# Cross-attention feeding a snake feed-forward layer: state times w_in formed per batch, blocks cut by batch, second layer and attention interleaved by hand

## The chip, the cores and the metric

The kernel runs on one core of one Trainium2 chip. The metric is the device time in microseconds of one execution. Matmuls run on PE (TensorE), whose weight loads are shown apart as PEld; elementwise work runs on DVE (VectorE), ACT (ScalarE) and POOL (GpSimd); transfers are started from the queues of POOL and SP. Each engine works through its own list of instructions in order and waits on semaphores of the others.

## What is computed

There are 8 batches b of 8 heads h; x[b, h] has 512 tokens of 64 numbers, state[b, h] has 32 rows of 64. Per head, attention runs both ways with the same scores, and the 512 + 32 results of all 8 heads are laid side by side as rows of 512 numbers. These 4352 rows go through a two-layer network.

```python
scores = scale * np.matmul(x, state.transpose(0, 1, 3, 2))
a = softmax(scores)                 # over the 32 state rows
xread = np.matmul(a, state)         # 512 x 64 per head
a2 = softmax(scores^T)              # over the 512 tokens
sread = np.matmul(a2, x)            # 32 x 64 per head
X = concat([xread, sread], axis=2)  # to 4352 rows of 512
h = X @ w_in                        # 512 -> 2048
g = h + sin(alpha * h)**2 / (alpha + 1e-09)
out = g @ w_out                     # 2048 -> 512, f32
```

## The kernel before

Everything inside is bf16 with f32 accumulation. Heads are worked on in pairs (q = 0 to 3; 2 x 64 = 128 partitions). Tokens of a batch lie four to a partition, so a batch is C = 4 chunks of 128 tokens. The intermediate X is kept transposed for all batches in `xT_all` [128, 4, 4352].

Loads: `load_batch` casts x to bf16 in flight (one transfer per batch on POOL's queue) and lays the state of a head pair out as a block diagonal `stbd` (a memset and two transfers per batch). w_in and w_out come as one transfer each. Transfers on POOL's queue use eight semaphores in turn, so from the ninth on each waits for the one eight before it.

Attention of a pair: `a1_transposes` copies x into pair order (`xp`, L116), transposes it and the state on PE; `a1_scores` copies the transpose out of PSUM (`xbT`, L130), makes the scores (L133) and their Exp on ACT (`E`, L140). `a2_rows` sums rows of E and divides on DVE (`R` L148, `rR` L150, `A` L153) and transposes A; `a2_readout` multiplies the state with it (`U_ps`, L170) and ACT casts the result into `xT_all` (L171). `a2_sread` makes x times E and, with a matrix of ones, the column sums (L181, L187), and DVE reduces, inverts and multiplies (L195 to L205).

The network: `moe_block` takes 512 columns of `xT_all`, whatever batch they are from: 8 blocks of 512 and one of 256. For each of 16 column tiles ft of w_in it runs four matmuls over the 512 rows (`hT_ps`, L259), Sin on ACT (L266), the square on POOL for even ft and on DVE for odd (L271), and one DVE instruction that scales the square and adds h from PSUM (`gT`, L274). Then each 128 rows of the block take 16 matmuls with w_out (`o_ps`, L283), a copy on ACT (L290) and stores from SP's queue.

`attn_a1(b + 1)`, `attn_a2(b)` and a block are written one after the other; the order in each engine's list is set by a scheduler with a cost model, which fills some instructions of neighbouring stages into each other. The pools set what may run ahead: four PSUM buffers `psumM` for `hT_ps`, scores, `U_ps` and `WTC_ps` together, two for transposes, two for `o_ps`.

Of the kernel before, what the change touches and what calls it, by code (L numbers as in the profile page):

```python
# [9 lines left out]
ACT = mybir.ActivationFunctionType  # L10
ALU = mybir.AluOpType
AX = mybir.AxisListType
BF16 = mybir.dt.bfloat16
FP32 = mybir.dt.float32


@with_exitstack
def kernel(
# [27 lines left out]
    bload = ctx.enter_context(tc.tile_pool(name="bload", bufs=B))
    epool = ctx.enter_context(tc.tile_pool(name="epool", bufs=2 * Q))
    pairp = ctx.enter_context(tc.tile_pool(name="pairp", bufs=3))
    smallp = ctx.enter_context(tc.tile_pool(name="smallp", bufs=4))
    moep = ctx.enter_context(tc.tile_pool(name="moep", bufs=2))  # L50
    outp = ctx.enter_context(tc.tile_pool(name="outp", bufs=2))
    psumT = ctx.enter_context(tc.tile_pool(name="psumT", bufs=2, space=bass.MemoryType.PSUM))
    psumM = ctx.enter_context(tc.tile_pool(name="psumM", bufs=4, space=bass.MemoryType.PSUM))
    psumO = ctx.enter_context(tc.tile_pool(name="psumO", bufs=2, space=bass.MemoryType.PSUM))

    ident = const.tile([P, P], BF16, name="ident")
    make_identity(nc, ident[:])
# [11 lines left out]
    xT_all = xt_pool.tile([P, Q, T_TOTAL], BF16, name="xT_all")

    xnat_l = [None] * B
    stbd_l = [None] * B

    def load_batch(b):
        xnat = bload.tile([P, H, C * D], BF16, name="xnat")
        nc.gpsimd.dma_start(
            xnat[:], x[b].rearrange("h (p i) d -> p h (i d)", i=C)
        )
        stbd = bload.tile([Ns * 2, Q, 2 * D], BF16, name="stbd")
        nc.gpsimd.memset(stbd[:], 0.0)  # L80
        stv = state[b].rearrange("(q r) j d -> r j q d", r=2)
        for r in range(2):
            nc.gpsimd.dma_start(
                stbd[r * Ns:(r + 1) * Ns, :, r * D:(r + 1) * D],
                stv[r],
            )
        xnat_l[b] = xnat
        stbd_l[b] = stbd

    load_batch(0)  # L90
    load_batch(1)
    w_in_sb = wpool.tile([P, Q, DFF], BF16, name="w_in_sb")
    nc.gpsimd.dma_start(w_in_sb[:], moe_w_in.rearrange("(q p) f -> p q f", p=P))
    for b in range(2, B):
        load_batch(b)
    w_out_sb = wpool.tile([P, FT, DOUT], BF16, name="w_out_sb")
    nc.gpsimd.dma_start(w_out_sb[:], moe_w_out.rearrange("(ft p) c -> p ft c", p=P))

    BLK = 512
    nblocks = (T_TOTAL + BLK - 1) // BLK  # L100

    ps = {}

    def a1_transposes(b, q):
        d = {}
        ps[(b, q)] = d
        xnat = xnat_l[b]
        stbd = stbd_l[b]
        stbdT_ps = psumT.tile([P, 2 * Ns], BF16, name="stbdT_ps", tag="tp")
        nc.tensor.transpose(stbdT_ps[:], stbd[:, q, :], ident[:Ns * 2, :Ns * 2])  # L110
        stbdT = pairp.tile([P, 2 * Ns], BF16, name="stbdT")
        nc.vector.tensor_copy(stbdT[:], stbdT_ps[:])  # L112
        d["stbdT"] = stbdT
        xp = pairp.tile([P, C, 2 * D], BF16, name="xp")
        for r in range(2):
            nc.vector.tensor_copy(  # L116
                xp[:, :, r * D:(r + 1) * D],
                xnat[:, 2 * q + r, :].rearrange("p (i d) -> p i d", i=C),
            )
        xbT_ps = psumT.tile([P, S], BF16, name="xbT_ps", tag="tp")  # L120
        for i in range(C):
            nc.tensor.transpose(  # L122
                xbT_ps[:, i * P:(i + 1) * P], xp[:, i, :], ident[:]
            )
        d["xbT_ps"] = xbT_ps

    def a1_scores(b, q):
        d = ps[(b, q)]
        xbT = pairp.tile([P, S], BF16, name="xbT")
        nc.vector.tensor_copy(xbT[:], d["xbT_ps"][:])  # L130
        S_ps = psumM.tile([P, C, 2 * Ns], FP32, name="S_ps", tag="hT")
        for i in range(C):
            nc.tensor.matmul(  # L133
                S_ps[:, i, :],
                xbT[:, i * P:(i + 1) * P],
                d["stbdT"][:],
                start=True, stop=True,
            )
# [156 lines left out]
    for b in range(B):  # L295
        if b + 1 < B:
            attn_a1(b + 1)
# [38 lines left out]
```

## Time and profile before

| | us |
|---|---|
| median of 3 runs | 372.04 |
| lowest and highest | 369.31, 373.11 |
| span of the profiled execution | 371.1 |

The profiled execution is one by itself, recorded apart from the three timed runs; of its time only the span, from the first instruction to the last, is on record, and it lies within the range of the runs.

How to read the page: the first part gives each engine's busy time and share of the span. In the part of 40 slices, each 9.28 us long, a digit is the busy share in tenths; the GB/s row is what the transfers moved. The chain that ended last is followed back from the last instruction through whatever released each step. A row of the groups gives line, engine, operation, out<-in by name, shape and count, then busy time, mean ns of one, idle time just before and what ended it. A row of the timeline gives start, duration, engine, line, operation and count, and in brackets the idle time before it and its releaser. A row by line gives the smallest, median and largest duration in ns. A row of the windows gives the stretch, its length, the busy time of PE, PEld, DVE, ACT and POOL with counts, then the granted TensorE clock (1.00 is full), the share of the DMA engines and GB/s.

### The profile page before, as it was taken

The numbers are of one execution on the slowest core, as the hardware profiler recorded it, in microseconds if no ns is written. First come the engines' busy times: TensorE is split into PE (matmuls) and PEld (weight loads), VectorE is DVE, ScalarE is ACT, GpSimd is POOL, SyncE is SP. The second block draws the span as 40 slices with busy tenths as digits, with TensorE's granted clock in tenths as the row PEclk, the third lists the DMA queues.
The fourth block names the chain that finished last, engine by engine and source line by source line (L and its number), as shares of the span: only waits on it lengthen the run. The fifth ranks groups of instructions, "written<-read, shape, count | busy, mean of one in ns | idle before, by whom it ended". The sixth has DMA issues, their size and how long they took to land.

```text
span 371.1 us, 5139 instructions
## 1 busy us (share of the span) xinstructions
PE 314.4 (85%) x1830; PEld 150.6 (41%) x1856; DVE 232.9 (63%) x602; ACT 160.5 (43%) x256; POOL 96.8 (26%) x113
## 2 busy tenths in 40 slices
PE   0458799989997989789997989789997999799994
PEld 0343334544343434443354434443453434334561
DVE  2657675289818991679627990789437970695081
ACT  1113362366334651556334641556254642363271
POOL 9238242015200440024200530025100430152040
PEclk9999989999998999989998999989998999899999
DMA  9999930200030002200120002000120003101201
GB/s 93 211 194 188 196 54 31 83 4 0 8 91 17 2 0 57 59 0 3 28 85 2 0 0 87 28 2 0 41 75 0 3 2 83 30 0 25 71 20 57
DMA packets 20681, 17.90 MB, mean 48 GB/s; under 512 B 5552, under 2 KB 15792, under 8 KB 20656
## 3 DMA queue, kind: packets, MB, share of 16 engines
q0 software_dynamic: 13216, 8.65, 16.1%
q1 hardware_dynamic: 7440, 8.93, 8.7%
q8 instruction: 14, 0.23, 0.2%
q14 instruction: 11, 0.09, 0.1%
HBM read 17.31 MB, written 8.91 MB: 71 GB/s over the span
## 4 chain that ended last, share of the span: by engine, by line
PE 47%; DVE 26%; POOL 12%; issue 6%; DMA 4%; ACT 3%; POOLq 0%; ACTq 0%
PE o_ps L283 25%; PE hT_ps L259 11%; POOL s_sb L271 10%; DVE gT L274 10%; DMA stbd<-in_state_dram 4%; DVE xbT L130 3%; PE U_ps L170 2%; DVE recipC L197 2%; DVE A L153 2%; PE WTC_ps L181 2%; DVE s_sb L271 2%; PE xbT_ps L122 2%; PE WTC_ps L187 2%; ACT s_sb L266 2%; DVE xp L116 2%
## 5 line engine op out<-in xcount | busy, mean ns | idle before, releaser
L259 PE MATMUL hT_ps<-xT_all,w_in_sb 128*128 128x512 bf16 (+1 forms) x560 | 138.7, 385 | 14.8 <-DVE gT L274 11.6
L271 POOL TENSOR_TENSOR s_sb<-s_sb 128x512 bf16<-128x512 bf16 (+1 forms) x72 | 74.2, 1031 | 250.5 <-ACT s_sb L266 175.2
L283 PE MATMUL o_ps<-w_out_sb,gT 128*128 128x512 bf16 x534 | 126.6, 379 | 2.7 <-DVE gT L274 2.0
L266 ACT ACTIVATE s_sb<-hT_ps,alpha_sb 128x512 bf16<-128x512 f32 (+1 forms) x144 | 94.7, 663 | 57.8 <-PE hT_ps L259 27.3
L274 DVE SCALAR_TENSOR_TENSOR gT<-s_sb,inva_sb,hT_ps 128x512 bf16<-128x512 bf16 (+1 forms) x144 | 101.5, 714 | 25.8 <-POOL s_sb L271 20.8
L259 PEld LDWEIGHTS <-w_in_sb 128*128 128x128 bf16 x576 | 58.0, 102 | 82.8 <-issue 34.8
L283 PEld LDWEIGHTS <-gT 128*128 128x128 bf16 x544 | 52.1, 98 | 68.8 <-DVE gT L274 9.6
L290 ACT COPY o_sb<-o_ps 128x512 f32<-128x512 f32 x34 | 19.9, 586 | 90.0 <-PE o_ps L283 86.4
L112 DVE COPY stbdT<-stbdT_ps 128x64 bf16<-128x64 bf16 x32 | 5.8, 182 | 57.6 <-PE stbdT_ps L110 46.6
L271 DVE TENSOR_TENSOR s_sb<-s_sb 128x512 bf16<-128x512 bf16 (+1 forms) x72 | 29.0, 402 | 0.0
L171 ACT CAST xT_all<-U_ps 128x512 bf16<-128x512 f32 x32 | 18.4, 592 | 21.4 <-PE U_ps L170 15.2
L130 DVE COPY xbT<-xbT_ps 128x512 bf16<-128x512 bf16 x32 | 13.5, 423 | 18.8 <-PE xbT_ps L122 17.5
L170 PE MATMUL U_ps<-AT,stbd 64*128 64x512 bf16 x32 | 13.3, 427 | 12.5 <-DVE AT L168 12.4
L195 DVE TENSOR_REDUCE Csum<-WTC_ps 128x64 f32<-128x256 f32 x32 | 13.3, 422 | 16.2 <-PE WTC_ps L187 15.6
L110 PE MATMUL stbdT_ps<-ident,stbd 64*128 64x64 bf16 x32 | 6.5, 204 | 16.9 <-DMA stbd<-in_state_dram 16.9
L140 ACT ACTIVATE E<-S_ps 128x256 bf16<-128x256 f32 x32 | 10.3, 388 | 22.8 <-PE S_ps L133 22.7
L116 DVE COPY xp<-xnat 128x256 bf16<-128x256 bf16 x64 | 17.5, 327 | 3.8 <-DMA xnat<-in_x_dram 3.4
L153 DVE TENSOR_TENSOR A<-E,rR 128x256 bf16<-128x256 bf16 x32 | 18.8, 591 | 0.0
L122 PE MATMUL xbT_ps<-ident,xp 128*128 128x128 bf16 x128 | 14.6, 242 | 4.0 <-DVE xbT L130 3.7
L197 DVE RECIPROCAL recipC<-Csum 128x64 f32<-128x64 f32 x32 | 15.3, 519 | 0.1
L266 ACT ACT_TABLE_LOAD x7 | 9.0, 1283 | 13.9 <-PE hT_ps L259 13.8
L168 DVE COPY AT<-AT_ps 64x512 bf16<-64x512 bf16 x32 | 13.1, 414 | 2.7 <-PE AT_ps L158 2.2
(30 smaller groups left out, 150.3 us busy)
## 6 DMA issues: line engine op xcount, KB each, us to landing
xnat<-in_x_dram POOLq DMA_DIRECT2D x8, 512.0 KB, 9.1
out_dram<-o_sb SPq DMA_DIRECT2D x16, 192.0 KB, 2.2
w_in_sb<-in_moe_w_in_dram POOLq DMA_DIRECT2D x1, 2048.0 KB, 16.1
w_out_sb<-in_moe_w_out_dram POOLq DMA_DIRECT2D x1, 2048.0 KB, 14.7
out_dram<-o_sb SPq DMA_DIRECT2D x8, 256.0 KB, 2.4
out_dram<-o_sb SPq DMA_DIRECT2D x16, 128.0 KB, 2.3
out_dram<-o_sb SPq DMA_DIRECT2D x24, 64.0 KB, 1.9
stbd<-in_state_dram POOLq DMA_DIRECT2D x16, 16.0 KB, 8.6
```

The lines of the kernel that those rows point to most:

```text
L116: nc.vector.tensor_copy(xp[:, :, r * D:(r + 1) * D], xnat[:, 2 * q + r, :].rearrange("p (i d) -> p i d", i=C),)
L122: nc.tensor.transpose(xbT_ps[:, i * P:(i + 1) * P], xp[:, i, :], ident[:])
L130: nc.vector.tensor_copy(xbT[:], d["xbT_ps"][:])
L153: nc.vector.tensor_tensor(A8, E8, rR[:].unsqueeze(2).to_broadcast([P, C * 2, Ns]), ALU.mult)
L170: nc.tensor.matmul(U_ps[:], stbd[:, q, :], AT[:], start=True, stop=True)
L197: nc.vector.reciprocal(recipC[:], Csum[:])
L259: nc.tensor.matmul(hT_ps[:, :Nt], w_in_sb[:, q, ft * P:(ft + 1) * P], xT_all[:, q, t0:t0 + Nt], start=(q == 0), stop=(q == Q - 1),)
L266: nc.scalar.activation(s_sb[:, :Nt], hT_ps[:, :Nt], ACT.Sin, scale=alpha_sb[:, ft:ft + 1])
L271: s2_eng.tensor_tensor(s2_sb[:, :Nt], s_sb[:, :Nt], s_sb[:, :Nt], ALU.mult)
L274: nc.vector.scalar_tensor_tensor(gT[:, ft, :Nt], s2_sb[:, :Nt], inva_sb[:, ft:ft + 1], hT_ps[:, :Nt], ALU.mult, ALU.add,)
L283: nc.tensor.matmul(o_ps[:tsz, :], gT[:, ft, st * P:st * P + tsz], w_out_sb[:, ft, :], start=(ft == 0), stop=(ft == FT - 1),)
L290: nc.scalar.copy(o_sb[:tsz], o_ps[:tsz])
```

## The change

The kernel is rewritten around one identity. For the token rows, h = (A state) w_in = A (state w_in). With M = state w_in for the 256 state rows of a batch (8 heads of 32; 256 x 2048), the first layer of a batch is A (512 x 256) times M: two matmuls per column tile of 512 tokens where there were four, and neither `U_ps` nor its cast is needed. M is formed per batch by 16 matmuls of 64 x 512 (`m_step`), copied to bf16 by ACT and DVE in turn. The 32 state rows of a batch have no such form; they are collected in `xs_all` for all batches and make a ninth block of 256 columns with the four matmuls of before.

A block is now a batch: blocks 0 to 7 have 512 tokens, block 8 the 256 state rows. The state comes in one transfer, is transposed once in `prep_state`, and kept as `stT` for all batches. w_in and w_out come in four transfers each and x of batch 0 in two. A's multiply and nearly all squares go to POOL; only the odd tiles of block 0 are squared on DVE. The column sums are added up in PSUM, so the reduction goes away.

The order is the written one (`manual_schedule`). In block t, slot f (0 to 15) holds: the two matmuls of the first layer of tile f with Sin and square; one piece of the list `fill` (attention and M of batch t + 1, then the state readout of batch t); the DVE combination of tile f - 1; and four matmuls of the second layer of block t - 1. The PSUM buffers are three for `h_ps`, two for `o_ps`, and three for all pieces of the list.

```diff
+    st_nat = const.tile([P, 16, D], BF16, name="st_nat")
+    nc.gpsimd.dma_start(st_nat[:], state.rearrange("b h (jh jl) d -> (b h jh) jl d", jl=16))
...
+    load_x(0, 2)
+    ident = const.tile([P, P], BF16, name="ident")
+    make_identity(nc, ident[:])
+    for k in range(FS):
+        nc.gpsimd.dma_start(
+            w_in_sb[:, :, k * FW:(k + 1) * FW], w_in_v[:, :, k * FW:(k + 1) * FW])
+    load_x(1, 1)
+    for k in range(4):
+        nc.gpsimd.dma_start(
+            w_out_sb[:, k * 4:(k + 1) * 4, :], w_out_v[:, k * 4:(k + 1) * 4, :])
+    for b in range(2, B):
+        load_x(b, 1)
...
+    def attn_steps(b, parts=1):
...
+        def p_step(k):
+            nc.vector.tensor_copy(a.xp[:, :, hs, :],
+                xnat_l[b][:, hs, :].rearrange("p h (i d) -> p i h d", i=C))
+        def t_step(qq):
+            if parts == 2 or qq == 0:
+                p_step(qq)
+            tp = psX.tile([P, 2, S], BF16, name="x_ps", tag="px")
...
+                    nc.tensor.transpose(...)
+            nc.vector.tensor_copy(a.xT[:, 2 * qq:2 * qq + 2, :], tp[:])
+        def s_step(ii):
+            sp = psX.tile([P, 2, H * Ns], FP32, name="s_ps", tag="px")
...
+            nc.scalar.activation(a.E[:, 2 * ii:2 * ii + 2, :], sp[:], ACT.Exp, scale=scale)
+        def r_step(ii):
+            nc.vector.reduce_sum(R, E8, axis=AX.X)
+            nc.vector.reciprocal(rR, R)
+            nc.gpsimd.tensor_tensor(
+                A8, E8, rR.unsqueeze(2).to_broadcast([P, 2 * H, Ns]), ALU.mult)
-        nc.vector.tensor_tensor(
-            A8, E8, rR[:].unsqueeze(2).to_broadcast([P, C * 2, Ns]), ALU.mult
-        )
+        def a_step():
+            tp = psX.tile([P, G, S], BF16, name="a_ps", tag="px")
...
+            nc.vector.tensor_copy(a.AT[:], tp[:])
+        return [lambda: t_step(0), lambda: t_step(1), lambda: s_step(0),
+            lambda: (s_step(1), r_step(0)), lambda: r_step(1), None, a_step]
+
+        def m_step(fs, g):
+            mp = psX.tile([P, FW], FP32, name="m_ps", tag="px")
+            for k in range(2):
+                q = 2 * g + k
+                nc.tensor.matmul(mp[k * 2 * Ns:(k + 1) * 2 * Ns, :],
+                    stT[:, b * G + g, k * 2 * Ns:(k + 1) * 2 * Ns],
+                    w_in_sb[:, q, fs * FW:(fs + 1) * FW], start=True, stop=True)
+            dst = M[:, g, fs * FW:(fs + 1) * FW]
+            if g == 0:
+                nc.scalar.copy(dst, mp[:])
+            else:
+                nc.vector.tensor_copy(dst, mp[:])
...
+        def c_step():
...
+            nc.vector.reciprocal(rC[:], cp[:])
+            for r in range(2):
+                nc.vector.tensor_tensor(xs_all[rows, :, b * Ns:(b + 1) * Ns],
+                    wp[rows, :, r * Ns:(r + 1) * Ns], rC[rows], ALU.mult)
+        return [lambda: w_step(0), lambda: (w_step(1), c_step())]
+
+    def mm1(t, f):
+        hp = psH.tile([P, S], FP32, name="h_ps")
+        if t < B:
+            for g in range(G):
+                nc.tensor.matmul(hp[:, :n], Ms[t][:, g, f * P:(f + 1) * P],
+                    atts[t].AT[:, g, :], start=(g == 0), stop=(g == G - 1))
...
+        nc.scalar.activation(s[:, :n], hp[:, :n], ACT.Sin, scale=alpha_sb[:, f:f + 1])
+        eng = nc.vector if (t == 0 and f % 2) else nc.gpsimd
+        eng.tensor_tensor(s2[:, :n], s[:, :n], s[:, :n], ALU.mult)
...
+    for t in range(B + 1):
+        if t + 1 < B:
+            an, mn = attn_steps(t + 1), m_steps(t + 1)
+            fill = [an[0], an[1], an[2], an[3], an[4], mn[0], an[6]] + mn[1:]
+        if t < B:
+            w = w_steps(t)
+            fill = (fill + w) if t + 1 < B else (w + fill)
+        for f in range(FT):
+            cur = mm1(t, f)
+            if fill[f]:
+                fill[f]()
+            if pend:
+                snake(*pend)
+            pend = (t, f) + cur
+            if t > 0:
+                mm2(t - 1, f // 4, (f % 4) * 4, (f % 4) * 4 + 4, box)
```

First place: POOL's list at the start, after the identity matrix is made; `DMASW0` to `DMASW7` are the eight semaphores of its transfers. Before, its last loads and its first elementwise work (the squares, L271):

```order
L83 DMA stbd<-in_state_dram 32x4x64 [waits DMASW6_49]
L80 MEMSET stbd 64x512
L97 DMA w_out_sb<-in_moe_w_out_dram 128x16x512 [waits DMASW7_49]
L83 DMA stbd<-in_state_dram 32x4x64 [waits DMASW0_49,Pool_49]
L83 DMA stbd<-in_state_dram 32x4x64 [waits DMASW1_49]
L271 TENSOR_TENSOR s_sb<-s_sb 128x512 [waits Activation_49]
```

Now, from the seventh load on, up to the first multiply for A (L185) and the first square (L296):

```order
L77 DMA xnat<-in_x_dram 128x8x256
L95 DMA w_out_sb<-in_moe_w_out_dram 128x4x512 [waits DMASW0_49]
L95 DMA w_out_sb<-in_moe_w_out_dram 128x4x512 [waits DMASW1_49]
L95 DMA w_out_sb<-in_moe_w_out_dram 128x4x512 [waits DMASW2_49]
L95 DMA w_out_sb<-in_moe_w_out_dram 128x4x512 [waits DMASW3_49]
L77 DMA xnat<-in_x_dram 128x8x256 [waits DMASW4_49]
L77 DMA xnat<-in_x_dram 128x8x256 [waits DMASW5_49]
L77 DMA xnat<-in_x_dram 128x8x256 [waits DMASW6_49]
L77 DMA xnat<-in_x_dram 128x8x256 [waits DMASW7_49]
L77 DMA xnat<-in_x_dram 128x8x256 [waits DMASW0_49]
L77 DMA xnat<-in_x_dram 128x8x256 [waits DMASW1_49]
L185 TENSOR_TENSOR A<-E,rR 128x512 [waits DVE_49,Activation_49] x2
```

Before, the multiply for A was on DVE and POOL's first work after the loads was a square of the first layer; now the multiply for A of batch 0, which the first layer of block 0 needs, stands behind all 18 loads.

Second place: ACT in a block, here block 1 and its counterpart before. Before (o_sb is the copy of the second layer's result, s_sb the Sin):

```order
L290 COPY o_sb<-o_ps 128x512 x4
L140 ACT_TABLE_LOAD
L140 ACTIVATE E<-S_ps 128x256 x4
L171 CAST xT_all<-U_ps 128x512 x4
L266 ACT_TABLE_LOAD
L266 ACTIVATE s_sb<-hT_ps,alpha_sb 128x512 x16
```

Now, from the Sin of slot 2 and those ahead of it to the first cast of M:

```order
L293 ACTIVATE s<-h_ps,alpha_sb 128x512 x6
L176 ACT_TABLE_LOAD
L176 ACTIVATE E<-s_ps 128x512
L293 ACT_TABLE_LOAD
L293 ACTIVATE s<-h_ps,alpha_sb 128x512
L176 ACT_TABLE_LOAD
L176 ACTIVATE E<-s_ps 128x512
L315 COPY o_sb<-o_ps 128x512
L293 ACT_TABLE_LOAD
L293 ACTIVATE s<-h_ps,alpha_sb 128x512 x2
L226 CAST M<-m_ps 128x512
```

Exp, which came in one run between two blocks with one table load on either side, now comes in two pieces among the Sin of slots 2, 3 and 4, with a load on either side of each.

Third place: the instructions around it on POOL and DVE in block 1 and its end. POOL before has only squares there. POOL now (s2 is the square; the squares are those of slots 2, 3, 4 and 5):

```order
L296 TENSOR_TENSOR s2_595<-s_593 128x512 [waits DVE_49,Activation_49]
L296 TENSOR_TENSOR s2_617<-s_615 128x512 [waits DVE_49,Activation_49]
L185 TENSOR_TENSOR A_539<-E_538,rR_542 128x512 [waits DVE_49,PE_49]
L296 TENSOR_TENSOR s2_645<-s_643 128x512 [waits Activation_49]
L185 TENSOR_TENSOR A_539<-E_538,rR_542 128x512 [waits DVE_49]
L296 TENSOR_TENSOR s2_661<-s_659 128x512 [waits Activation_49]
```

DVE before, where the copy xp (L116) is made head by head among the combinations (L274) and squares (L271):

```order
L271 TENSOR_TENSOR s_sb<-s_sb 128x512
L116 COPY xp<-xnat 128x4x64
L274 SCALAR_TENSOR_TENSOR gT<-s_sb,inva_sb,hT_ps 128x512 x2
L271 TENSOR_TENSOR s_sb<-s_sb 128x512
L116 COPY xp<-xnat 128x4x64
L274 SCALAR_TENSOR_TENSOR gT<-s_sb,inva_sb,hT_ps 128x512
L112 COPY stbdT<-stbdT_ps 128x64
```

DVE now, from the end of block 1 into block 2 (the combinations are those of slots 14 and 15 of block 1 and slots 0 and 1 of block 2):

```order
L264 RECIPROCAL rC<-c_ps 128x128
L267 TENSOR_TENSOR xs_all<-w_ps,rC 64x4x32 x2
L300 SCALAR_TENSOR_TENSOR gT<-s_819,inva_sb,h_ps 128x512
L146 COPY xp<-xnat 128x2048
L163 COPY xT<-x_ps 128x1024
L300 SCALAR_TENSOR_TENSOR gT<-s_840,inva_sb,h_ps 128x512
L163 COPY xT<-x_ps 128x1024
L300 SCALAR_TENSOR_TENSOR gT<-s_885,inva_sb,h_ps 128x512
L300 SCALAR_TENSOR_TENSOR gT<-s_909,inva_sb,h_ps 128x512
```

On POOL the two multiplies for A moved in between the squares. On DVE the copy xp of a whole batch is one instruction behind the state readout of the batch before, at the point where PE's transposes of slot 0 need it.

More of the change, by code (lines that the diff above doesn't have):

```diff
@@ L69 @@
[L69 to L85, printed above, removed]
-            )
-        xnat_l[b] = xnat
-        stbd_l[b] = stbd
@@ L90 @@
[L90 to L118, printed above, removed]
-            )
[L120 to L138, printed above, removed]
-        E = epool.tile([P, C, 2 * Ns], BF16, name="E")
-        nc.scalar.activation(E[:], S_ps[:], ACT.Exp, scale=scale)
-        d["E"] = E
@@ L163, in a2_readout @@
[L163 to L180 removed]
+    w_in_sb = wpool.tile([P, Q, DFF], BF16, name="w_in_sb")
@@ L181, in a2_sread @@
+    def mm1(t, f):
+        n = S if t < B else B * Ns
+        hp = psH.tile([P, S], FP32, name="h_ps")
+        if t < B:
+            for g in range(G):
                 nc.tensor.matmul(
[L182 to L192 removed]
@@ L309 @@
+    snake(*pend)
+    for st in range(B * Ns // P):
+        for k in range(4):
+            mm2(B, st, 4 * k, 4 * k + 4, box)
 _INS = ['x', 'state', 'moe_w_in', 'moe_w_out', 'moe_alpha']
```

367 lines of the change are left out of this document (204 added, 163 removed).

## The prediction

> **What bounds the kernel now.** I read the page from the top, then the groups by shape, the timeline of PE with its waits, and the granted clock in short windows.
>
> ```profile
> span 371.1 us, 5139 instructions
> PE 314.4 (85%) x1830; PEld 150.6 (41%) x1856; DVE 232.9 (63%) x602; ACT 160.5 (43%) x256; POOL 96.8 (26%) x113
> PE   0458799989997989789997989789997999799994
> GB/s 93 211 194 188 196 54 31 83 4 0 8 91 17 2 0 57 59 0 3 28 85 2 0 0 87 28 2 0 41 75 0 3 2 83 30 0 25 71 20 57
> PE 47%; DVE 26%; POOL 12%; issue 6%; DMA 4%; ACT 3%; POOLq 0%; ACTq 0%
> ...
> 35.25 0.63 PE L259 MATMUL hT_ps<-xT_all,w_in_sb 128*128 128x512 bf16 x1
> ...
> 198.96 0.40 PE L170 MATMUL U_ps<-AT,stbd 64*128 64x512 bf16 x1 [1.80 <-DVE AT L168]
> 240.10 0.59 PE L170 MATMUL U_ps<-AT,stbd 64*128 64x512 bf16 x1 [1.79 <-DVE AT L168]
> ...
> 340.48 0.59 ACT L290 COPY o_sb<-o_ps 128x512 f32<-128x512 f32 x1 [2.56 <-PE o_ps L283]
> 343.93 0.59 ACT L290 COPY o_sb<-o_ps 128x512 f32<-128x512 f32 x1 [2.87 <-PE o_ps L283]
> ```
>
> PE is the busiest engine, yet only 47% of the chain that ended last; the rest runs through DVE, POOL and ACT. The kernel is a bare PE stage (second layer) alternating with a latency-bound one (attention, first layer). Two neighbouring output copies in the bare stage are 3.45 us apart for 16 matmuls: 0.216 us per 128x512 matmul. The same U_ps matmul recurs 41.1 us later: the period for 512 tokens. The first first-layer matmul stands at 35.25.
>
> **PE work of the change.**
>
> ```profile
> 232.79 0.40 PE L133 MATMUL S_ps<-stbdT,xbT 128*128 128x64 bf16 x8
> 233.26 0.40 PE L122 MATMUL xbT_ps<-ident,xp 128*128 128x128 bf16 x4
> 82.70 0.75 DVE L274 SCALAR_TENSOR_TENSOR gT<-s_sb,inva_sb,hT_ps 128x512 bf16<-128x512 bf16 x1 [0.93 <-POOL s_sb L271]
> 83.50 1.02 PE L259 MATMUL hT_ps<-xT_all,w_in_sb 128*128 128x512 bf16 x4 [1.12 <-DVE gT L274]
> ```
>
> A group's duration holds about 0.2 of latency: 64-wide matmuls follow at about 0.03, 128-wide ones at about 0.056; four 512-wide ones end after 1.02, so two after 0.60; a released engine starts 0.05 to 0.09 later. Per batch the first layer falls from 64 matmuls to 32 (0.43 per slot, a slot being one of 16 column tiles f) and 16 are added to form M; 0.86 of second layer joins each slot. So 16 x 1.30 = 20.8. The fills: slots 0 and 1 eight transposes (0.45 each), 2 and 3 scores (0.23), 5 and 7 to 13 M (0.43), 6 the transposes of A (0.45), 14 and 15 0.23 and 0.68. Sum 6.1; a batch needs 26.9 us of PE. The two M matmuls write different halves of the partitions; no row shows whether they overlap, so a pair costs 0.22 to 0.43; I take 0.43, as all 512-wide rows queue up.
>
> **The waits that interleaving makes.** Every engine keeps program order, and h_ps has three buffers: slot f+3 waits for the DVE combination of f.
>
> ```profile
> L266 ACT ACTIVATE s_sb<-hT_ps,alpha_sb 128x512 bf16<-128x512 f32 x128 | 87.2, 687 | 55.2 <-PE hT_ps L259 26.7 <-DVE s_sb L271 15.8 <-POOL s_sb L271 7.7
> L271 POOL TENSOR_TENSOR s_sb<-s_sb 128x512 bf16<-128x512 bf16 x64 | 69.3, 1083 | 231.7 <-ACT s_sb L266 161.3 <-DVE gT L274 43.1 <-DVE xbT L130 24.8
> L274 DVE SCALAR_TENSOR_TENSOR gT<-s_sb,inva_sb,hT_ps 128x512 bf16<-128x512 bf16 x128 | 93.8, 744 | 12.1 <-POOL s_sb L271 7.8
> L171 ACT CAST xT_all<-U_ps 128x512 bf16<-128x512 f32 x32 | 18.4, 592 | 21.4 <-PE U_ps L170 15.2 <-PE stbdT_ps L110 5.9
> L130 DVE COPY xbT<-xbT_ps 128x512 bf16<-128x512 bf16 x32 | 13.5, 423 | 18.8 <-PE xbT_ps L122 17.5
> L112 DVE COPY stbdT<-stbdT_ps 128x64 bf16<-128x64 bf16 x32 | 5.8, 182 | 57.6 <-PE stbdT_ps L110 46.6
> L197 DVE RECIPROCAL recipC<-Csum 128x64 f32<-128x64 f32 x32 | 15.3, 519 | 0.1
> L205 DVE TENSOR_TENSOR xT_all<-WTC_ps,recipC 64x32 bf16<-64x32 f32 x32 | 6.2, 194 | 0.4
> L148 DVE TENSOR_REDUCE R<-E 128x8 f32<-128x256 bf16 x32 | 12.3, 389 | 0.2 <-ACT E L140 0.2
> L150 DVE RECIPROCAL rR<-R 128x8 f32<-128x8 f32 x32 | 6.1, 195 | 0.1
> L116 DVE COPY xp<-xnat x64: 175/220/1064, 7.7 to 245.5; 128x256 bf16<-128x256 bf16 x64
> L153 DVE TENSOR_TENSOR A<-E,rR x32: 406/416/1262, 17.4 to 292.9; 128x256 bf16<-128x256 bf16 x32
> L140 ACT ACTIVATE E<-S_ps 128x256 bf16<-128x256 f32 x32 | 10.3, 388 | 22.8 <-PE S_ps L133 22.7
> ...
> 72.12 0.59 ACT L290 COPY o_sb<-o_ps 128x512 f32<-128x512 f32 x1 [2.87 <-PE o_ps L283]
> 72.72 1.28 ACT L140 ACT_TABLE_LOAD   x1
> 74.02 1.21 ACT L140 ACTIVATE E<-S_ps 128x256 bf16<-128x256 f32 x4
> ```
>
> Sizes that no row has, from these (ends in brackets): xT and AT copies of 1024, 0.70, by the slope between 0.182 for 64 and 0.423 for 512; row sum of 512, 0.63 (0.39 to 0.78); reciprocal of 128, 0.88, by the slope from 0.195 to 0.519; a product of 128 for xs, 0.3 (0.19 to 0.78); Exp of 512, 0.60 (0.39 to 0.69); xp of 2048 in one piece, 0.65 (0.22 to eight times 0.22 = 1.8), and it starts behind a running POOL operation: the like copy's longest is 1.06 against a median of 0.22. The cast of M on DVE, 0.60, as on ACT (0.42 to 0.75). A's multiply moves to POOL with an f32 operand; I take the square's 1.08 (from 0.42, DVE's for half the size, to 2.2, twice the square).
>
> Now walk blocks 1 to 6, T counted from the start of the slot 15 ahead of one.
> - Slot 0. PE ends slot 15 at 1.98 and matmul 0 at 2.41; its transposes need xp, which on DVE stands behind the reciprocal (1.33 to 2.21), two xs products (to 2.85) and combination 14 (to 3.60). POOL squares from 3.42 to 4.51, so xp runs from 4.5 to 5.2. PE stands 2.8. Slot 1 then starts at 6.55, slot 2 at 8.28.
> - Slots 2 to 4, ACT: Sin 2 ends 9.63; load, Exp, load (12.8); Sin 3 to 13.5; load, Exp (15.4), output copy, load (17.24); Sin 4 to 17.9, Sin 5, a cast of M. The row sum waits for the first Exp, combination 2 stands behind it and ends at 13.2: slot 5 is late by 0.6. The second sum holds combination 3 until 17.05: slot 6 is late by 2.1.
> - Slot 6: the transposes of A wait for POOL: square 4 (18.0 to 19.1), then the second multiply, 20.2. PE, at 17.53, stands 2.7. Slot 7 starts at 21.55, and from there POOL (1.08 per 1.73 slot), ACT and DVE keep up: slot 15 starts at 35.2.
>
> So 2.8 + 0.6 + 2.1 + 2.7, about 8.3 us of stalls, on 26.9. The squares, the casts of M and the output copies cost nothing beside: per batch POOL has 18 x 1.08 = 19.5, ACT 11.0 of Sin, 1.2 of Exp, 5.1 of loads and 4.7 of copies = 22, DVE 11.9 of combinations, 2.4 of casts and 5.9 of the rest = 20, all under 26.9. Were PE faster, ACT would be late next, then DVE and POOL.
>
> **The clock** is the next term.
>
> ```profile
> 82.00:84.00 2.00, 0.88 (x9) 0.52 (x7) 1.29 (x3) 0.86 (x3) 1.07 (x2) 1.00 0.00 0
> 240.00:242.00 2.00, 1.90 (x20) 1.06 (x21) 1.39 (x6) 0.59 (x1) 0.00 (x0) 0.54 0.00 0
> 242.00:244.00 2.00, 1.78 (x6) 0.68 (x6) 1.83 (x7) 0.18 (x1) 0.00 (x0) 0.61 0.03 8
> ```
>
> After the 1.79 us gap at 240 the granted clock is 0.54 and 0.61 for 4 us, a loss of 1.7 us; after the 1.12 gap at 83.5 it stayed 1.00. In the change the gaps around slot 6 (2.1 and 2.7 with little between) should bring one such dip per block; the 2.8 gap lies between dense work, and I give it none. So 35.2 + 1.7 = 36.9, with 35.2 and 38.6 as ends. The Trainium skill ("TensorE: Matmul & The Clock Gate", Part 1) says the clock is halved after an idle window of about 3.4 us; by that rule no gap here would do it and the sum would be 10 lower, and the trace, where 1.79 us among light work sufficed, does not agree.
>
> **Head, block 0, tail.**
>
> ```profile
> 22.11 1.10 POOL L83 DMA_DIRECT2D stbd<-in_state_dram  x2 [7.54 <-DMA w_in_sb<-in_moe_w_in_dram]
> ...
> 363.27 3.40 PE L283 MATMUL o_ps<-w_out_sb,gT 128*128 128x512 bf16 x15 [0.55 <-DVE gT L274]
> ...
> 366.71 0.59 ACT L290 COPY o_sb<-o_ps 128x512 f32<-128x512 f32 x1 [2.65 <-PE o_ps L283]
> 367.68 0.43 SPq L246 DMA_DIRECT2D out_dram<-o_sb  x1
> ```
>
> POOL issues all 18 loads before its first multiply, and from the ninth each waits for the load eight earlier, as here for w_in. The last waits for the second quarter of w_out: ahead of it 0.26 (state) + 0.52 + 2.10 + 0.52 + 1.05 = 4.46 MB in bf16. The GB/s row (slices of 9.28 us) reaches 3.5 MB at 22.1, where 3.2 had to be there, so I take 0.3 more: 4.76 MB at 28.6. Issue 0.9, two multiplies 2.2, transposes 0.65, AT 0.7 and the handovers: first-layer matmul at 33.3 (before 35.25; alone, the data would allow some 10 earlier).
> Block 0 has no second layer. The same ACT chain gives slot 7 at 14.1; then a pair of slots takes matmul 0.65, Sin 0.75, square on DVE 0.45, M cast 0.6, combination 0.75 = 3.2, and slot 15 starts at 27.2.
> Block 7, with no attention to fill in, is bare PE: 20.8 + 0.9 = 21.7. Block 8 (256 state tokens, four matmuls at 0.108 per slot) 20.7. The last 32 second-layer matmuls 6.9. From the last matmul's end (366.67) to the span's end 4.4, and three more stores at about 0.45 each: 5.8.
> Sum: 33.3 + 27.2 + 6 x 36.9 + 2.0 + 21.7 + 20.7 + 6.9 + 5.8 = 339.0, against the span 371.1; the median of the runs, 372.04, is 0.9 above that span, so 340.
>
> **Rivals.**
> 1. The stalls are hidden, because the walk is too strict (xp or the multiply earlier, M pairs overlapping): 6 x 26.9 in place of 6 x 36.9 gives 280; half of it 310. For it: ACT, DVE and POOL have 5 us or more to spare per block; against it: strict order and three buffers. 0.25.
> 2. A table switch costs more than its row. The change has 28 loads on the chain in blocks 0 to 6; at twice 1.28 each they add 36: 376, slower by 1%. Against it: the load at 72.72 follows a copy at once, and Exp starts 0.02 after its end. 0.03. The Trainium skill ("ScalarE: Activation LUTs", What ACT_TABLE_LOAD costs) adds a drain of about 1380 ns to each switch, which would make it an estimated 379; the 0.02 does not agree.
> 3. Slower: POOL's multiply by an f32 broadcast is slow. From 3.3 us on both multiplies lie in series ahead of the transposes of A; at 4.9 each a block loses the 5.3 us that make up 372, and at 6.0 the time is 340 + 6 x 7.5 = 385. Against it: the square's 1.08. 0.05.
>
> **How the numbers follow.** The forecast has 0.67. Its own ends: no dip -10, xp without POOL -6, M pairs overlapping in six open slots -8, against a second dip +10, the multiply at 2.2 +7, xp at 1.8 +7; not all at once: 316 to 362. Rival 1 is taken in down to 305; what lies outside is its lower part, rivals 2 and 3: 2 in 10. A measurement here tells apart about 1%, 3.7 us: faster 0.89 (rival 1 and the forecast but for its upper tail), same 0.03 (that tail), slower 0.08 (rivals 2 and 3).
>
> **What would show it.** Right: 28 table loads in pairs around Exp behind Sin; per block three gaps of PE, before x_ps (waiting for xp), before h_ps in slot 6 (gT) and before a_ps (POOL's A), 8 us together; first h_ps at about 33; a period of 37; a clock dip behind a_ps. Wrong: a period near 27 with PE gapless; POOL's A far over 1.1; first h_ps before 25 or after 40; a dip at every gap.

## The result and the profile after

The changed kernel takes 350.66 us (median of 4 runs, 349.87 to 351.36), against 372.11 (369.31 to 373.11) for the kernel before beside it. The ratio is 0.943 with a 95% interval of 0.938 to 0.948. The forecast was 340, with a range of 305 to 362: the direction is right and the time lies in the range, but the kernel is 10.7 us slower than forecast.

From the page of the changed kernel: the span, busy times, two of the rows in 40 slices (here 8.69 us each) and the shares of the chain.

```profile
span 347.7 us, 4220 instructions
PE 269.5 (78%) x1536; PEld 119.7 (34%) x1536; DVE 178.1 (51%) x285; ACT 174.5 (50%) x256; POOL 165.3 (48%) x176
PE   2515478695997689776979599749978699999993
PEclk9999855587898969996998789987989699999998
PE 56%; ACT 15%; DVE 9%; issue 7%; POOL 6%; DMA 5%; ACTq 0%; POOLq 0%
```

From the waits of PE in the same kernel: how long it waited in all, how often, and the longest.

```profile
PE a_ps L193 <- POOL A L185: 24.8, 9, 10.3
PE h_ps L282 <- DVE gT L300: 20.6, 19, 3.7
PE x_ps L158 <- DVE xp L146: 19.7, 9, 3.1
```

PE has 45 us less to do than before, but only 23.4 us of that came off the span. PE's three largest waits are at the three places that the prediction named, 65 us in all (10.3 of it once, in the head), and the PEclk row shows what it had put at one dip per block: the clock is at 0.5 to 0.8 from slice 5 to 9 and falls again in nearly every block after that. Slot 15 of the blocks 0 to 6 starts at 61.85, 101.81, 139.97, 177.02, 215.09, 252.13 and 290.19 on PE's timeline, which makes 38.06 us per block (228.34 / 6). The three gaps, in PE's timeline of block 2:

```profile
106.90 1.03 PE L158 MATMUL x_ps<-ident,xp 128*128 128x128 bf16 x8 [2.51 <-DVE xp L146]
...
116.36 0.59 PE L282 MATMUL h_ps<-AT,M 128*128 128x512 bf16 x2 [0.41 <-DVE gT L300]
...
120.27 1.01 PE L282 MATMUL h_ps<-AT,M 128*128 128x512 bf16 x2 [2.01 <-DVE gT L300]
...
123.29 0.82 PE L193 MATMUL a_ps<-ident,A 128*128 128x128 bf16 x6 [1.80 <-POOL A L185]
```

Together 6.7 us. What follows them is in the windows of 2 us (length, busy time of PE, PEld, DVE, ACT and POOL, granted clock, DMA share, GB/s):

```profile
118.00:120.00 2.00, 0.26 (x2) 0.00 (x0) 1.29 (x3) 1.97 (x4) 0.85 (x1) 1.00 0.02 6
120.00:122.00 2.00, 1.23 (x4) 0.40 (x3) 0.22 (x1) 1.99 (x4) 0.81 (x1) 0.55 0.33 125
122.00:124.00 2.00, 0.71 (x7) 0.71 (x8) 0.75 (x1) 0.76 (x2) 2.00 (x3) 0.50 0.00 0
124.00:126.00 2.00, 2.00 (x7) 0.67 (x5) 1.35 (x2) 0.00 (x0) 1.23 (x2) 0.50 0.00 0
126.00:128.00 2.00, 2.00 (x8) 0.54 (x7) 0.75 (x2) 0.69 (x1) 0.46 (x1) 0.74 0.04 8
```

The pair of gaps (2.01 and 1.80, with 1.2 us of PE work between) is followed by about 7 us of half clock. As a measure of what that takes, I add up over windows of 0.5 us PE's busy time times one minus the granted clock; it is called clock loss below. For the changed kernel it is 30.8 us (before: 11.2): 2.3 to 2.4 at the long dip of each of the blocks 1 to 6, 1.5 at a shorter one behind the 2.51 us gap in blocks 2, 4 and 6 (in 3 and 5 the same gap leaves the clock at 1.00; the last section shows why), and 11.9 in one stretch from 41.7 to 72.4, which is block 0 and the start of block 1. The trace has no reading of the clock ahead of 34.88, and the page takes it as 1.00 there; eight transposes for x_ps take 1.03 us at 33.40 and 0.61 at 34.99, so it was lower.

### The profile page after: what moved, and what is told of

It is laid out like the page before. It is cut to its first block, busy times and chain, and to the rows that moved or that the text cites. A ratio compares the mean times of both kernels' runs of the same rounds, so it can differ in the third digit from the quotient of the medians.

```text
span 347.7 us, 4220 instructions
## 1 busy us (share of the span) xinstructions
PE 269.5 (78%) x1536; PEld 119.7 (34%) x1536; DVE 178.1 (51%) x285; ACT 174.5 (50%) x256; POOL 165.3 (48%) x176
## 4 chain that ended last, share of the span: by engine, by line
PE 56%; ACT 15%; DVE 9%; issue 7%; POOL 6%; DMA 5%; ACTq 0%; POOLq 0%
PE o_ps L309 30%; PE h_ps L282 13%; ACT L293 5%; DMA w_out_sb<-in_moe_w_out_dram 5%; PE m_ps L218 5%; ACT L176 4%; ACT s L293 4%; PE x_ps L158 3%; POOL A L185 3%; DVE xp L146 3%; DVE gT L300 2%; PE h_ps L288 2%; DVE rC L264 2%; PE a_ps L193 2%; ACT o_sb L315 1%
## 5 line engine op out<-in xcount | busy, mean ns | idle before, releaser
L296 POOL TENSOR_TENSOR s<-s 128x512 bf16<-128x512 bf16 (+1 forms) x136 | 134.2, 989 | 153.0 <-ACT s L293 147.3
L293 ACT ACTIVATE s<-h_ps,alpha_sb 128x512 bf16<-128x512 f32 (+1 forms) x144 | 94.9, 664 | 118.6 <-PE h_ps L282 107.7
L309 PE MATMUL o_ps<-w_out_sb,gT 128*128 128x512 bf16 x544 | 149.3, 402 | 0.0
L300 DVE SCALAR_TENSOR_TENSOR gT<-s,inva_sb,h_ps 128x512 bf16<-128x512 bf16 (+1 forms) x144 | 100.7, 705 | 37.3 <-POOL s L296 36.4
L282 PE MATMUL h_ps<-AT,M 128*128 128x512 bf16 x256 | 87.2, 426 | 20.6 <-DVE gT L300 20.6
L282 PEld LDWEIGHTS <-M 128*128 128x128 bf16 x256 | 25.8, 104 | 57.2 <-issue 34.8
L228 DVE CAST M<-m_ps 128x512 bf16<-128x512 f32 x32 | 22.0, 687 | 34.3 <-PE m_ps L218 34.3
L218 PE MATMUL m_ps<-w_in_sb,stT 128*64 128x512 bf16 x128 | 29.9, 479 | 0.2 <-ACT M L226 0.2
L158 PE MATMUL x_ps<-ident,xp 128*128 128x128 bf16 x128 | 13.2, 265 | 19.7 <-DVE xp L146 19.7
L226 ACT CAST M<-m_ps 128x512 bf16<-128x512 f32 x32 | 18.6, 580 | 13.5 <-PE m_ps L218 13.5
L185 POOL TENSOR_TENSOR A<-E,rR 128x512 bf16<-128x512 bf16 x16 | 16.9, 1059 | 4.3 <-DVE rR L184 4.3
```

The costliest lines, as they stand in the source:

```text
L158: nc.tensor.transpose(tp[:, k, i * P:(i + 1) * P], a.xp[:, i, 2 * q:2 * q + 2, :].rearrange("p r d -> p (r d)"), ident[:],)
L185: nc.gpsimd.tensor_tensor(A8, E8, rR.unsqueeze(2).to_broadcast([P, 2 * H, Ns]), ALU.mult)
L218: nc.tensor.matmul(mp[k * 2 * Ns:(k + 1) * 2 * Ns, :], stT[:, b * G + g, k * 2 * Ns:(k + 1) * 2 * Ns], w_in_sb[:, q, fs * FW:(fs + 1) * FW ...
L228: nc.vector.tensor_copy(dst, mp[:])
L282: nc.tensor.matmul(hp[:, :n], Ms[t][:, g, f * P:(f + 1) * P], atts[t].AT[:, g, :], start=(g == 0), stop=(g == G - 1),)
L293: nc.scalar.activation(s[:, :n], hp[:, :n], ACT.Sin, scale=alpha_sb[:, f:f + 1])
```

## The experiments

Every kernel was timed against the kernel before in the same series. All edits are on the changed kernel. The last column but one is the distance of slot 15 of block 6 from that of block 0, by six.

| | median us | ratio to before, 95% | us per block | clock loss us |
|---|---|---|---|---|
| changed kernel | 350.66 | 0.943 (0.938 to 0.948) | 38.06 | 30.8 |
| warm | 331.27 | 0.892 (0.887 to 0.897) | 34.83 | 2.7 |
| xp_early | 327.58 | 0.882 (0.878 to 0.886) | 34.12 | 25.7 |
| exp_pair | 324.34 | 0.873 (0.867 to 0.879) | 33.86 | 9.2 |
| a_late | 325.05 | 0.874 (0.869 to 0.878) | 34.37 | 15.5 |
| all3 | 294.57 | 0.793 (0.789 to 0.797) | 29.21 | 7.6 |
| head | 337.83 | 0.909 (0.904 to 0.913) | 38.01 | 29.8 |
| best | 282.78 | 0.762 (0.757 to 0.767) | 29.21 | 3.8 |
| best_warm0 | 281.12 | 0.760 (0.753 to 0.767) | 29.22 | 0.0 |
| apart | 374.50 | 1.010 (1.007 to 1.013) | 39.66 | 30.7 |
| four | 349.09 | 0.941 (0.938 to 0.944) | 37.08 | 15.4 |
| best_four | 305.06 | 0.820 (0.817 to 0.824) | 31.85 | 7.8 |

The traces of xp_early and all3 have readings from about 19 us on, and so their clock loss holds 2.8 and 3.0 us of the head, which that of the changed kernel leaves out.

**warm: is it the clock?** The theory: the walk of the prediction (35.2 us per block) is right, and what is above it is the halved clock. The rival: the walk is too short and the clock is only a companion. The edit fills the gaps of blocks 1 to 6 with matmuls whose result nothing reads.

```diff
             cur = mm1(t, f)
+            if 1 <= t <= 6 and f in (0, 6):
+                filler(10 if f == 0 else 8)
             if fill[f]:
...
                 mm2(t - 1, f // 4, (f % 4) * 4, (f % 4) * 4 + 4, box)
+            if 1 <= t <= 6 and f == 5:
+                filler(8)
```

> The changed kernel with work added: in blocks 1 to 6 PE runs 10, 8 and 8 matmuls of no use (their result is not read) where it stands in slot 0, ahead of slot 6 and ahead of the transposes of A; gaps, order and all else stay. Theory (half the cost of the stalls is the clock that falls after them): no dip is left in blocks 1 to 6, the period falls from 38.0 to about 34, and the kernel is faster by 15 to 24 us: 327 to 336. Rival (the gaps alone cost the time, the clock loss lies in their shadow): 350 or slower, as PE gets 5.6 us more work per block.

Measured: 331.27, inside the theory's bounds. 26 more matmuls per block make the kernel 19.4 us faster. The clock row of this kernel's page:

```profile
PEclk9999958999999999999999999999999999999999
```

And the window of one block of it, from one x_ps to the next:

```profile
101.40:136.29 34.89, 33.00 (x199) 14.63 (x203) 20.66 (x31) 20.97 (x30) 18.55 (x18) 1.00 0.08 31
```

The clock stays at 1.00 and the block takes 34.89 us, against the 35.2 of the walk. Per block that is 3.23 us less than the changed kernel, and six times 3.23 is the whole 19.4. This is the run that settles the main question. It doesn't settle block 0, which has no filler here: its half clock ended at 51.2 instead of 72.4, and from slot 9 on two slots take 3.15 us instead of 3.56; but slot 7 had come a microsecond later than in the changed kernel, so that slot 15 starts at 61.80 against 61.85.

**xp_early, exp_pair, a_late, all3: the three waits.** Each takes away the cause of one wait. xp_early makes the copy xp of batch t + 2 in slot 10 of block t, away from the state readout and one block before it is needed. exp_pair puts both Exp of a batch into slot 2, so that ACT switches tables once there and back, and the row sums into slots 3 and 4. a_late moves the transposes of A from slot 6 to slot 9, behind four pieces of M. all3 does all of it. The core of xp_early (`xp_ahead` makes the copy that `p_step` made):

```diff
+            if f == 10 and t + 2 < B:
+                xp_ahead(t + 2)
```

> The copy xp of batch t+2 moves from the start of block t+1 to slot 10 of block t (batches 2 to 7). Theory (PE stands in slot 0 for xp, and all behind it shifts): the 2.5 us gap before x_ps goes in blocks 1 to 6 (15 us), with it the clock dip that followed it in about half of them (1.6 us each): 331 us, range 326 to 337. Rival (ACT and POOL set the end of each block anyway, PE waits longer at h_ps instead): 350 us, the h_ps waits grow by 2.5 per block.

Measured: 327.58, within the expectation. PE's waits fall where they should and nowhere else:

```profile
PE a_ps L193 <- POOL A L185: 24.7, 9, 10.3
PE h_ps L282 <- DVE gT L300: 20.9, 19, 4.1
PE x_ps L158 <- DVE xp L146: 4.6, 3, 3.1
```

Of the 23.1 us gained, 15.1 are the wait itself (19.7 - 4.6) and 7.9 the clock: without the 2.8 of the head, 22.9 us of clock loss stand against 30.8. The dips ahead of x_ps are gone; the long dip stays in blocks 3 to 6 and is half as long in 1 and 2.

The edit of exp_pair:

```diff
-            lambda: s_step(0),
-            lambda: (s_step(1), r_step(0)),
+            lambda: (s_step(0), s_step(1)),
+            lambda: r_step(0),
             lambda: r_step(1),
```

> Both score steps of a batch in slot 2, so that the two Exp stand side by side: 2 table loads per block in place of 4. Theory (the loads delay Sin 3 and Sin 4, DVE waits for Exp): the gap before slot 6 falls from 2.0 to under 1, POOL's second multiply comes earlier, 1 to 3 us per block: 338 us, range 330 to 345. A rival by which a table switch costs twice its row would give twice the ACT time back, 14 switches fewer x 2.6: under 330. If ACT is off the path: 350.

Measured: 324.34, faster than its bounds, so the expectation was wrong in size. The gaps that stay, in PE's timeline of one block of exp_pair:

```profile
100.64 0.62 PE L158 MATMUL x_ps<-ident,xp 128*128 128x128 bf16 x8 [2.51 <-DVE xp L146]
...
108.62 0.59 PE L282 MATMUL h_ps<-AT,M 128*128 128x512 bf16 x2 [0.41 <-DVE gT L300]
...
111.43 0.59 PE L282 MATMUL h_ps<-AT,M 128*128 128x512 bf16 x2 [0.91 <-DVE gT L300]
...
113.66 0.82 PE L193 MATMUL a_ps<-ident,A 128*128 128x128 bf16 x6 [1.52 <-POOL A L185]
```

The pair around slot 6 went from 3.81 to 2.43 us, a mere 1.4; but a block became 4.2 us shorter. The rest goes with the clock (loss 9.2 instead of 30.8): the pair, shortened this much, brought a dip in three of the six blocks, and the gap ahead of x_ps, still 2.51 in most, none from block 2 on. So part of this gain hangs on where the gaps fall in the beat that the last section shows, and the four runs, 322.3 to 327.0, rank with their granted clock, 0.965 to 0.935. The time also meets the rival's "under 330" for a table switch that costs twice its row; the gaps, which shrank by 1.4 us only, and ACT's rows further below speak against it.

The edit of a_late:

```diff
-            fill = [an[0], an[1], an[2], an[3], an[4], mn[0], an[6]] + mn[1:]
+            fill = [an[0], an[1], an[2], an[3], an[4]] + mn[:4] + [an[6]] + mn[4:]
```

> The transposes of A move from slot 6 to slot 9, four M steps ahead of them. Theory (PE stands behind POOL's multiply): the gap before a_ps of 1.8 to 2.3 us goes in blocks 0 to 6, and the long clock dip gets shorter: 335 us, range 328 to 340. Rival (the time is taken back at the next h_ps, since POOL is behind with its squares too): 348 to 350.

Measured: 325.05, again more than expected, for the same reason: with the 1.80 us gap gone the 2.01 us gap beside it is alone, and the dip of 6.8 us becomes one of 3.4 (1.6 lost). The dips of blocks 2, 4 and 6 ahead of x_ps are gone too, though their gap is 2.51 as before: again a matter of where it falls.

> The three edits together. Theory: per block only some 1 us of gaps is left, no dip, period 27 to 29 in place of 38: 290 us, range 283 to 305, and the granted clock in blocks 1 to 6 near 1.00. Rival (a second limit beneath, ACT or POOL): sum of the single gains or less, 315 to 330.

Measured: 294.57, as expected. The window of one block:

```profile
102.55:131.70 29.15, 27.62 (x176) 12.16 (x176) 19.77 (x31) 18.38 (x29) 19.01 (x19) 1.00 0.10 37
```

PE is busy 27.6 of 29.15 us at full clock; gaps of 0.41 and 0.91 are left. Alone, the three edits gain 23, 26 and 26 us, 75 in all; together they gain 56. The clock accounts for the difference: the clock loss that the three take away alone adds up to 45 us (7.9, 21.6 and 15.3), but all3, without the 3.0 of its head, takes away only 26. The 19 us between are loss that more than one edit removes, and it can be gained only once.

**head, best, best_warm0: the start.** head takes the loads of x for batches 2 to 7 out of POOL's list at the start and gives each out at the start of a block. best is all3 with head; best_warm0 adds filler matmuls in block 0. The edit of head:

```diff
-    for b in range(2, B):
-        load_x(b, 1)
...
+        for b in ((2, 3) if t == 0 else (t + 3,)):
+            if b < B:
+                load_x(b, 1)
```

> The loads of x for batches 2 to 7 move behind POOL's multiplies of batch 0, into the blocks (two ahead). Theory (POOL's list holds the first layer back): the first h_ps at 21 to 23 in place of 31.9, 9 to 10 us: 341 us, range 338 to 344. Rival (w_in or x of batch 1 lands too late, or block 0 starts with a colder clock and gives it back): 346 to 351.

Measured: 337.83, 0.2 us better than the bounds. POOL's timeline of the changed kernel, and then that of head:

```profile
27.19 0.87 POOL L77 DMA_DIRECT2D xnat<-in_x_dram  x1 [1.67 <-DMA w_out_sb<-in_moe_w_out_dram]
28.08 2.06 POOL L185 TENSOR_TENSOR A<-E,rR 128x512 bf16<-128x512 bf16 x2
```

```profile
17.02 1.05 POOL L183 TENSOR_TENSOR A<-E,rR 128x512 bf16<-128x512 bf16 x1 [4.59 <-DVE rR L182]
18.43 1.05 POOL L183 TENSOR_TENSOR A<-E,rR 128x512 bf16<-128x512 bf16 x1 [0.36 <-DVE rR L182]
```

In the changed kernel the multiply starts when the issue of the last load, which had waited for a quarter of w_out, is over. In head it waits for its own operand instead and comes 11 us earlier. The first matmul of the first layer starts at 21.29, not 31.94, and 12.8 us come off the time.

> The three edits for the gaps and the moved loads together. Theory: 294.6 less 9 to 10: 285 us, range 281 to 289. Rival (the loads, now issued among POOL's squares, hold the squares up and open gaps in the blocks): 292 or more.

Measured: 282.78, as expected: 0.762 of the kernel before.

The edit of best_warm0, behind the four matmuls of the second layer, which block 0 has not:

```diff
             if t > 0:
                 mm2(t - 1, f // 4, (f % 4) * 4, (f % 4) * 4 + 4, box)
+            elif f >= 4:
+                filler(12 if f == 4 else 2)
```

> The one before with matmuls of no use in block 0: 12 at the end of slot 4, 2 at the end of each later slot. Theory (block 0 runs at half clock, as PE has too little to do there, and its chain holds matmuls): the clock is 1.00 from slot 5 on and 2 to 5 us are gained: 280 to 283. Rival (block 0 is set by DVE and ACT, or the clock does not rise for so little work): no gain, or up to 5 us slower.

Measured: 281.12. The clock did rise: from the first h_ps to slot 15 block 0 takes 25.1 us, where best takes 27.0 (20.89 to 46.02 and 20.83 to 47.85 on PE's timelines). But the intervals of the two ratios overlap, so the 1.7 us of the medians stay unconfirmed.

**apart, four, best_four: which part of the change pays?** apart keeps M and all else, but writes the second layer of a block behind it instead of into the slots of the next.

```diff
-            if t > 0:
-                mm2(t - 1, f // 4, (f % 4) * 4, (f % 4) * 4 + 4, box)
-    snake(*pend)
+        snake(*pend)
+        pend = None
+        for st in range(C if t < B else B * Ns // P):
+            for k in range(4):
+                mm2(t, st, 4 * k, 4 * k + 4, box)
```

> The changed kernel without the interleaving of the second layer: its 64 matmuls of a block run in one piece behind slot 15 (block 8's too); attention and M stay among the slots. Theory (the four matmuls per slot fill time in which PE would wait for ACT, POOL and DVE): a block costs a first-layer stage of 24 to 30 us and 14 us of bare matmuls, period 38 to 44, total 360 to 385. Rival (forming M alone brought the gain, the interleaving little): 345 to 355.

Measured: 374.50, within the theory's bounds and 1.0% slower than the kernel before. The waits of PE on the combination DVE makes rise from 20.6 us to this:

```profile
PE h_ps L282 <- DVE gT L300: 52.4, 58, 3.7
```

So without the interleaving the change gains nothing, the halved first layer included: in this order the first layer, bare, waits for DVE's combination. The gain of 21 us hangs on the interleaving.

four takes the other part away, as far as PE's load goes: four matmuls per slot instead of two, and no M formed after batch 0, whose M stands in for all. The casts of M on ACT and DVE go with it.

```diff
-            for g in range(G):
+            gs = [0, 1] if t == 0 else [0, 1, 0, 1]
+            for k, g in enumerate(gs):
                 nc.tensor.matmul(
-                    hp[:, :n], Ms[t][:, g, f * P:(f + 1) * P], atts[t].AT[:, g, :],
-                    start=(g == 0), stop=(g == G - 1),
+                    hp[:, :n], Ms[0][:, g, f * P:(f + 1) * P], atts[t].AT[:, g, :],
+                    start=(k == 0), stop=(k == len(gs) - 1),
...
-            an, mn = attn_steps(t + 1), m_steps(t + 1)
+            an, mn = attn_steps(t + 1), [None] * 8
```

> The changed kernel without M for batches 1 to 7: the M steps are left out, and the first layer of blocks 1 to 7 runs four matmuls per slot, with batch 0's M twice over (the readout of the old form, four matmuls per batch, is left out too). PE has 6.9 us more of first layer and 3.5 us less of M per block. Theory (PE carries a block where it does not stand): 2 to 4 us per block more, less what the gaps take up: 355 to 375. Rival (the stalls and the clock set the blocks, M pays little): 345 to 353.

Measured: 349.09, which the rival expected and the theory did not: the same as with M. PE gets more work per block, but its gaps shrink (x_ps 1.23, h_ps 1.72) and the clock loss halves. In the changed kernel as it stands, forming M pays nothing on balance. How much of that is PE's work lying in the shadow of its waits, and how much the casts that four saves ACT and DVE, this run doesn't separate.

> The version with the gaps closed and the loads moved, again without M for batches 1 to 7 (four matmuls per slot with batch 0's M, no M steps, no old readout). Theory (M pays nothing while PE stands and its clock falls, and pays its PE work once PE carries the blocks): the period rises from 29.2 by 2.5 to 3.4, total 298 to 306. Rival (M pays nothing here either, since ACT, POOL or the order set the period): 283 to 288.

Measured: 305.06, as expected; one block of best_four:

```profile
65.34:97.03 31.69, 30.62 (x188) 15.09 (x192) 17.42 (x27) 16.68 (x24) 19.47 (x20) 1.00 0.24 51
```

PE is busy 30.6 of 31.7 us. Now each slot costs what its matmuls cost, and the form with M is 22 us faster (282.78). The kernel before's old readout (`U_ps` and its cast) isn't in four and best_four, so the worth of M against the full old form was not measured.

## Why the prediction was right, and where it was off

- **The gaps: right in place and cause, a little too large.** Forecast 2.8, 0.6, 2.1 and 2.7 us per block, measured 2.51, 0.41, 2.01 and 1.80 to 2.32. xp_early and a_late took away the first and the last alone, and the others stayed: the causes are those named.
- **The walk without a dip: right in sum, in part by luck.** 35.2 forecast, 34.8 in warm. The gaps had been taken about 1 us too long (8.2 against 6.7 to 7.3) and PE's work about as much too short: a block of all3 takes 29.15 with 1.3 of gaps, so 27.8 of work, where the sum had 26.9.
- **The clock: the term that was mis-sized.** The prediction gave one dip of 1.7 us per block and none to the 2.8 us gap ahead of x_ps. Measured: a block takes 38.06, and 34.83 in warm, so the clock costs 3.2 us per block. Against the 36.9 of the forecast that is 1.16 too much, six times, or 6.9 us of the 10.7. The dip behind a_ps is 6.8 us long and loses 2.4, because two gaps stand close together; the gap ahead of x_ps, between dense work, does bring a dip in half the blocks (1.5). With the start of block 1, still at half clock from block 0 (4.0), the clock loss of the six blocks is 22.9 us. They are 19.4 us longer than in warm (228.3 - 209.0), so some 3.5 us of the loss cost no time, presumably because PE would have waited there anyway. The prediction's upper end had a second dip in it, and so its range held the time.
- **Block 0: 2.7 us too short.** Its slot 15 comes 29.9 us behind the first h_ps, not 27.2 (its own terms, 14.1 and four pairs of 3.2, make 26.9). Slot 7 is at 15.6 instead of 14.1, and a pair of slots from there takes 3.58 (14.31 / 4), not 3.2. The pairs' part goes with the clock, which the prediction left at 1.00 in block 0: in warm, once it is back, a pair takes 3.15. Why slot 7 is late stays open; in warm it comes a microsecond later still.
- **The head: 1.4 us early.** 31.94 instead of 33.3. That the last loads hold it was right, as head shows.
- **Block 7, block 8 and the tail** came out at 24.1, 20.8, 7.0 and 5.6, against 23.7, 20.7, 6.9 and 5.8. A last 2.0 us of the 10.7 lie between span and time: the median is 3.0 us above the profiled span, where the prediction took 0.9. Each of the four runs lies 2.1 to 2.2 above its own span, and the profiled one (349.87) was the fastest of them.
- **M pairs: right sum, wrong reason.** A slot with M was costed without overlap of its two matmuls. PE's timeline shows that they do overlap (0.41 for the two, against 0.59 for two that fill all columns) and the slot takes 1.74 all the same:

```profile
128.01 0.59 PE L282 MATMUL h_ps<-AT,M 128*128 128x512 bf16 x2
128.54 0.41 PE L218 MATMUL m_ps<-w_in_sb,stT 128*64 128x512 bf16 x2
128.88 1.04 PE L309 MATMUL o_ps<-w_out_sb,gT 128*128 128x512 bf16 x4
129.75 0.59 PE L282 MATMUL h_ps<-AT,M 128*128 128x512 bf16 x2
```

  The step from h_ps to m_ps is 0.53, where between full-width groups it is 0.43, and from m_ps to o_ps 0.34, together 0.87 like two steps of full width: what the overlap gains is given back at the switch of width. That is a reading of starts; no run tested it alone.
- **Rivals.** The first (stalls hidden) was wrong for this order of the program but right for what the order could be: all3 came to 294.6 with three small moves. The second (a costlier table switch) and the third (a slow multiply on POOL) are out: ACT's timeline has a load follow a Sin and an Exp follow the load at once, with 1.28 each, and the multiply takes 1.05 (head's rows above).

```profile
112.14 0.69 ACT L293 ACTIVATE s<-h_ps,alpha_sb 128x512 bf16<-128x512 f32 x1 [1.05 <-PE h_ps L282]
112.84 1.28 ACT L176 ACT_TABLE_LOAD   x1
114.14 0.60 ACT L176 ACTIVATE E<-s_ps 128x512 bf16<-128x512 f32 x1
114.75 1.28 ACT L293 ACT_TABLE_LOAD   x1
```

## What to carry to other kernels

A wait of PE of about 2 us can cost more than itself: price the half clock behind it in steps of 3.41 us, price gaps that stand close together as one longer gap, and let the range hold both cases, that a gap falls inside a step and that it falls across two. Fewer matmuls need not pay while another engine's order sets the pace (four); settle first who makes PE wait (here three pieces that were written one or a few slots too close to their use), then count matmuls. And a compute engine whose queue also issues loads should get its first work ahead of every load that may wait.

## What the runs showed of the hardware

- **Useless matmuls can pay.** 26 matmuls per block that nothing reads made the kernel 5.5% faster (350.66 to 331.27), by the clock alone.
- **Half clock can last.** In the changed kernel it stayed at 0.50 from 41.7 to 72.4 us, although PE was busy 3.4 to 3.6 us of every 4 from 48 to 64. Windows of 4 us:

```profile
48.00:52.00 4.00, 3.59 (x10) 0.66 (x8) 3.47 (x6) 1.85 (x3) 0.94 (x1) 0.50 0.01 1
...
68.00:72.00 4.00, 4.00 (x20) 2.07 (x18) 1.55 (x3) 0.69 (x1) 0.23 (x1) 0.50 0.02 4
72.00:76.00 4.00, 4.00 (x33) 2.07 (x32) 1.81 (x3) 2.48 (x3) 1.85 (x2) 0.95 0.00 0
```

  It came back behind 3.4 us without any gap (69.0 to 72.4). The Trainium skill ("TensorE: Matmul & The Clock Gate", Part 1) asks for a busy window of about 3.4 us for that, and the trace agrees, though in block 2 a little less was enough (3.07 of 3.41 us, the row from 106.56 below). Its idle window of the same length for the way down doesn't fit the gaps of 2.5 us and less behind which the clock was halved here.
- **The clock moves on a beat of 3.41 us.** In the changed kernel, up to the last matmul, the half clock lasts 30.72 us once, 6.83 six times and 3.41 three times, which is nine, two and one times 3.413, and its starts (41.70, 82.67, 106.56, 120.21 and so on) lie whole multiples of that apart. How busy PE was in one step shows in the clock of the next. Here are the steps around the gap of 2.51 us ahead of x_ps, which in block 2 lies almost wholly inside one step (104.39 to 106.90, first row) and in block 3 across two (142.54 to 145.05, last two rows):

```profile
103.14:106.56 3.42, 1.25 (x6) 0.39 (x4) 3.34 (x5) 1.23 (x3) 2.08 (x2) 1.00 0.20 77
106.56:109.97 3.41, 3.07 (x14) 1.70 (x15) 1.63 (x3) 0.00 (x0) 0.00 (x0) 0.50 0.00 0
...
140.69:144.10 3.41, 1.85 (x18) 0.76 (x14) 2.84 (x5) 1.84 (x3) 1.98 (x3) 1.00 0.15 57
144.10:147.52 3.42, 2.47 (x24) 1.65 (x25) 2.31 (x4) 0.46 (x1) 0.34 (x1) 1.00 0.05 20
```

  Blocks 4 and 6 are like block 2, block 5 like block 3. So the same gap costs a dip or none by where it falls, which the prediction's walk left out. How empty a step must be is not settled by the busy time alone: in exp_pair one with 1.44 us of PE work (229.31 to 232.73) brought no dip, and in the changed kernel one with 1.53 (266.98 to 270.40) did.
- **DVE's copy behind a POOL operation.** The copy xp takes 0.685 us where POOL is quiet (smallest and median in all3). At 143.46 in the changed kernel it started 0.06 after a square on POOL and took 1.53. DVE's timeline, and then POOL's:

```profile
143.46 1.53 DVE L146 COPY xp<-xnat 128x2048 bf16<-128x2048 bf16 x1
```

```profile
143.40 1.04 POOL L296 TENSOR_TENSOR s<-s 128x512 bf16<-128x512 bf16 x1 [0.94 <-ACT s L293]
```

  It ended 0.55 us behind the square. The Trainium skill ("SBUF — State Buffer", SBUF: two separate sides) tells of a port that the two share and that blocks the later one outright; the two rows agree nearly, since a copy begun only behind the square would have ended 0.685 behind it.
